# First transform of a folded FNet block: mirror sums at the norm, one pass for mirrored rows, a list by readiness, modulation by products

## The chip, the cores and the metric

The kernel runs on one core of a Trainium2 chip. The core has five engines with queues of their own: TensorE (PE, matrix products into PSUM), VectorE (DVE), ScalarE (ACT), GpSimd (POOL) and SyncE (SP, which issues most transfers). Transfers run on 16 DMA engines that all queues share. The metric is the device time in microseconds; lower is better.

## The reference

One block of a network on x (2048 rows, 512 columns), all in float32:

```python
sa, ca, ga, sb, cb, gb = (silu(c) @ w_mod).reshape(6, 512)
h = layernorm(x) * (1 + ca) + sa
a, b = h @ Wd_re.T, h @ Wd_im.T                 # 512 x 512, "hidden" transform
x = x + ga * (Ws_re @ a - Ws_im @ b)            # 2048 x 2048, "sequence" transform
h = layernorm(x) * (1 + cb) + sb
x = x + gb * ((silu(h @ w1) * (h @ w3)) @ w2)   # 1792 wide
```

The matrices Ws and Wd are those of a Fourier transform, so rows and columns have mirror images: cosines are even, sines odd. The kernel uses this (it folds rows and their mirrors together), checks on the way that the matrices given are of that kind, and has a general program behind a branch for the case that they are not.

## The kernel before, in words

The function `folded` is the main program. Tiles are taken from 50 slots of 4 KB per partition (`take`, `give`, first in, first out). Each product in full precision is three products of split operands (`PASSES`: high x high, high x low, low x high), where ScalarE rounds the high part (`copy`, L85) and VectorE makes the low part by a subtraction (`minus`, L88).

*Loads.* SyncE issues them in this order: the condition c, x rows of k = 0, the matrix of the modulation's scale (v = 1), x of k = 1, the matrix of its shift (v = 0), the four blocks of the two hidden matrices (`load_hid`, L225), x of k = 2 and 3. The rows of x are taken in eight steps k of 256: 128 rows and their 128 mirrors (`load_x`, L203 to L205; from k = 4 on the mirrors come by an indirect transfer that GpSimd issues, L168). An issue waits when eight transfers of the queue are on their way.

*Modulation.* ScalarE scales half of each matrix row by silu(c) (`copy_by`, L317), VectorE adds the other half (L292), and TensorE sums over the partitions with a column of ones (L301). This is done for four tiles, two for each of scale and shift; `mod_end` (L310) brings the sums to SBUF.

*First transform,* by k. The norm's statistics (L424, L425), root (L429), and scaling of the two tiles of rows (L444, L449); eight transposes (L464) into four PSUM banks that two k share; the modulation on the way out of PSUM (L477, L479); high and low part of the transposed rows of two k (`split_rows`). Then the hidden transform of 128 rows and of their 128 mirrors apart, in two banks (`hid_product`, L502: 24 products of 512 columns per k, three passes; `hid_odd` copies -2 times the state in between; `hid_difference`, L531: 8 products of 512 columns). Sums and differences of the two banks are taken afterwards on VectorE (`mirror_sums`, `hid_low_rows`, `hid_high_rows`), and their high and low parts are made: `us`, `ul` from the sums, `uh` from the mirrors' rows alone, of which only the high part is used. The order is written out by hand in the loop over k with the table STEPS.

*Second transform and the rest.* `seq_unit` multiplies `us`, `ul`, `uh` with the prepared blocks of the sequence matrices (L657, 32 units of 24 products). The first unit holds the last steps of the first transform (`last_rows`). Their blocks are loaded by `load_some` (L587) and prepared by `prepare_seq`. The two layers of the feed-forward part follow (L98), then the outputs' stores (L1048) and the branch to the general program.

Of the kernel before, what the change touches and what calls it, by code (L numbers as in the profile page):

```python
# [42 lines left out]
def folded(nc, pools, c, cp, wmr, wmc, x, xt, ctr, cti, wdr, wdi, w1, w3, w2, out):  # L43

# [184 lines left out]
    load_wm(1)  # L229
    load_x(1)  # L230
    load_wm(0)
# [53 lines left out]
    mod_acc = bank(6)  # L285

    def mod_scale(v):

        for h in range(2):
            w = wm[v, h]  # L290
            copy_by(w[:, 0, :], w[:, 0, :], sc[:, 2 * h : 2 * h + 1])
            nc.vector.scalar_tensor_tensor(  # L292
                w[:, 0, :], w[:, 1, :], sc[:, 2 * h + 1 : 2 * h + 2], w[:, 0, :],
                op0=OP.mult, op1=OP.add,
            )

    def mod_sum(v):

        for dt in range(ND):
            for h in range(2):  # L300
                nc.tensor.matmul(  # L301
                    mod_acc[:, v * ND + dt : v * ND + dt + 1],
                    hid_cols(wm[v, h][:, 0, :], dt),
                    onesf[:, :1],
                    start=h == 0,
                    stop=h == 1,
                )

    def mod_end(v):
        nc.vector.tensor_scalar(  # L310
            mod1[:, v, :], mod_acc[:, v * ND : (v + 1) * ND], float(v), None, op0=OP.add
        )
        for h in range(2):
            give(wm.pop((v, h)))
# [55 lines left out]
    wt, wu, wd = {}, {}, {}  # L370

    def prepare_w(dt):
# [5 lines left out]

        minus(u[:, 1, 0, :], r[:, 0, 0, :], u[:, 0, 0, :].bitcast(F32))
# [3 lines left out]
        )  # L383

# [34 lines left out]
    def norm_stats(k):  # L419
        mv = small.tile([P, 2, 2], F32, name=f"mv_{k}", tag="mv")  # L420
        rs[k] = mv, small.tile([P, 3, 2], F32, name=f"rs_{k}", tag="rs")
        for side in range(2):
            st = small.tile([P, 6], F32, name=f"st_{k}_{side}", tag="st")
            nc.vector.bn_stats(st, xz[k][:, side, :])  # L424
            nc.vector.bn_aggr(mv[:, side, :], st)  # L425
# [5 lines left out]
    def norm_scale(k):  # L431

        mv, r = rs.pop(k)
        by_scalar = (0, 1) if k in (2, 3, 4, 5) else (1,)
        nc.vector.reciprocal(r[:, 1, :], r[:, 0, :])
        first = by_scalar[0]
        nc.vector.tensor_tensor(
            out=r[:, 2, first:], in0=mv[:, first:, 0], in1=r[:, 1, first:], op=OP.mult
        )
        nc.vector.tensor_scalar(r[:, 2, first:], r[:, 2, first:], -1.0, None, op0=OP.mult)  # L440
        for side in range(2):
            a = xz[k][:, side, :]
            if side in by_scalar:
                nc.scalar.activation(  # L444
                    a, a, AF.Identity, bias=r[:, 2, side : side + 1],
                    scale=r[:, 1, side : side + 1],
                )
            else:
                nc.vector.tensor_scalar(  # L449
                    a, a, mv[:, side, 0:1], r[:, 1, side : side + 1],  # L450
                    op0=OP.subtract, op1=OP.mult,
                )


    turned = {}
    hm, hh, hl = {}, {}, {}

    def turn_rows(k):
        g, p = divmod(k, 2)
        if p == 0:  # L460
            turned[g] = [bank(dt) for dt in range(ND)]
# [1800 lines left out]
```

## Time and profile before

| | us |
|---|---|
| median of 3 runs (726.54 to 727.52) | 726.9 |
| the profiled execution | 725.83 |
| its span in the profile | 723.9 |
| first product of the second transform | 99.4 |
| second transform without a break from | 104.8 |
| TensorE busy | 695.6 |
| VectorE busy | 551.8 |
| ScalarE busy | 431.8 |

The profile takes one execution apart. "Busy" counts the time in which an engine has at least one instruction under way; products are pipelined, so that the busy time of one is longer than its distance to the next. Groups give line, engine, operation, output and inputs by their names, shape, count, then busy us and mean ns, then the idle time ahead of them with what ended it. Stretches give each engine's busy time with its instructions in brackets, TensorE's granted clock, the share of the 16 DMA engines and GB/s. The chain of waits goes back from the last instruction to what released each one; its pieces count only the time that a step adds to the chain.

### The profile page before, as it was taken

To read this page: it belongs to the slowest core of one execution; us is meant where nothing else is said; L and a number is where in the kernel's file an instruction comes from. 1 tells how busy PE (TensorE), PEld (TensorE's weight loads), DVE (VectorE), ACT (ScalarE), POOL (GpSimd) and SP (SyncE) were. 2 spreads that over 40 slices of the span, in tenths; PEclk is the share of its full clock that TensorE was granted. 3 is DMA by queue.
4 is the path that set the end of the run, shared out by engine and by line. 5 is a ranking of instruction groups with operands and counts; after the bars stand their busy time and mean duration, and the time that the engine had idled before them with its cause. 6 is when DMAs were issued, how large, how long until landed. Compare 5 with 4: busy or idle time off the path is not lost.

```text
span 723.9 us, 8651 instructions
## 1 busy us (share of the span) xinstructions
PE 695.6 (96%) x3018; PEld 562.6 (78%) x3018; DVE 551.8 (76%) x881; ACT 431.8 (60%) x684; POOL 128.2 (18%) x147
## 2 busy tenths in 40 slices
PE   7978989999999999989999999999999999999994
PEld 4666868878888888868888788777788888888784
DVE  5767788999899989758997987897666456664763
ACT  4668767535544575457566767777575655756330
POOL 2602044353343200010101001011010101101000
PEclk8889999999999999999999999999999999999998
DMA  7703059878587642162468575456944648447503
GB/s 240 225 0 117 0 173 314 313 234 317 203 294 255 237 135 70 31 115 88 74 189 163 138 166 99 104 91 144 289 87 117 146 76 185 87 90 151 141 0 121
DMA packets 37955, 108.91 MB, mean 150 GB/s; under 512 B 4880, under 2 KB 5136, under 8 KB 37904
## 3 DMA queue, kind: packets, MB, share of 16 engines
q0 software_dynamic: 12352, 43.00, 28.5%
q1 hardware_dynamic: 25552, 65.29, 27.0%
q8 instruction: 25, 0.41, 0.2%
q14 instruction: 26, 0.21, 0.1%
HBM read 76.81 MB, written 33.55 MB: 152 GB/s over the span
## 4 chain that ended last, share of the span: by engine, by line
PE 74%; DVE 11%; ACT 7%; DMA 3%; issue 2%; SPq 2%; ACTq 0%; DVEq 0%
PE bank L98 50%; PE bank L657 22%; DMA wmr<-in_wmr 1%; ACT xc L801 1%; PE bank L531 1%; DVE hl L88 1%; ACT hm L479 1%; SPq L225 1%; ACT us L85 1%; DVE xc L94 1%; PE bank L502 1%; DVE up L88 1%; DVE up L91 1%; ACT x L444 1%; ACT hf L85 1%
## 5 line engine op out<-in xcount | busy, mean ns | idle before, releaser
L98 PE MATMUL bank<-hf,w2h 128*128 128x512 f32 (+1 forms) x452 | 140.8, 391 | 0.3
L1053 POOL DMA_DIRECT2D sum<-y x48 | 41.1, 855 | 388.9 <-ACT y L317 371.8
L98 PEld LDWEIGHTS bank<-hf,w2h 128*128 128x128 f32 x452 | 84.3, 188 | 22.2 <-DVE hf L88 3.4
L98 PE MATMUL bank<-hf,w2l 128*128 128x512 f32 (+1 forms) x226 | 87.6, 388 | 0.0
L85 ACT ACTIVATE hf<-v 128x512 fp32r<-128x512 f32 x56 | 35.3, 630 | 67.7 <-DVE v L94 63.1
L317 ACT ACTIVATE y<-bank,gb 128x512 f32<-128x512 f32 x96 | 64.8, 682 | 18.1 <-PE bank L98 17.6
L91 DVE TENSOR_TENSOR v<-bank,x 128x512 f32<-128x512 f32 x36 | 24.7, 685 | 34.6 <-PE bank L98 34.6
L168 POOL DMA_INDIRECT re<-in_ctr,mirror x32 | 36.1, 1127 | 82.4 <-ACT junk L186 32.1
L657 PE MATMUL bank<-bh,us 128*128 128x512 f32 x128 | 49.9, 390 | 0.4 <-DVE xr L712 0.4
L657 PE MATMUL bank<-bh,ul 128*128 128x512 f32 x128 | 49.8, 389 | 0.0
L657 PE MATMUL bank<-l,us 128*128 128x512 f32 x128 | 49.8, 389 | 0.0
L657 PE MATMUL bank<-d,us 128*128 128x512 f32 x128 | 49.8, 389 | 0.0
L657 PE MATMUL bank<-d,uh 128*128 128x512 f32 x128 | 49.8, 389 | 0.0
L657 PE MATMUL bank<-l,uh 128*128 128x512 f32 x128 | 49.8, 389 | 0.0
L91 DVE TENSOR_TENSOR x<-bank,x 128x512 f32<-128x512 f32 x36 | 24.7, 687 | 32.4 <-PE bank L98 28.7
L98 PEld LDWEIGHTS bank<-hf,w2l 128*128 128x128 f32 x226 | 42.4, 188 | 8.3
L88 DVE TENSOR_TENSOR hf<-v,hf 128x512 fp32r<-128x512 f32 x56 | 38.4, 686 | 12.4 <-ACT hf L85 12.4
L502 PE MATMUL bank<-wu,hh 128*128 128x512 f32 x128 | 42.7, 416 | 4.9 <-ACT hh L85 3.8
L1131 ACT ACTIVATE v<-v 128x512 f32<-128x512 f32 x36 | 22.8, 632 | 38.6 <-DVE v L91 38.6
L85 ACT ACTIVATE x<-bank 128x512 f32<-128x512 f32 x72 | 41.4, 586 | 7.1 <-PE bank L98 6.5
L168 POOL DMA_INDIRECT im<-in_cti,mirror x32 | 34.4, 1076 | 35.4 <-DVE l L88 9.8
L502 PEld LDWEIGHTS bank<-wu,hh 128*128 128x128 f32 x128 | 24.8, 197 | 12.3 <-ACT hh L85 4.7
(233 smaller groups left out, 1772.0 us busy)
## 6 DMA issues: line engine op xcount, KB each, us to landing
sum<-y POOLq DMA_DIRECT2D x48, 512.0 KB, 5.4
w<-in_w SPq DMA_DIRECT2D x42, 512.0 KB, 4.7
re<-in_ctr SPq DMA_DIRECT2D x32, 256.0 KB, 4.9
im<-in_cti SPq DMA_DIRECT2D x32, 256.0 KB, 4.6
wmc<-in_wmc SPq DMA_DIRECT2D x8, 512.0 KB, 6.5
xr<-in_xt SPq DMA_DIRECT2D x8, 512.0 KB, 7.9
sum<-xr SPq DMA_DIRECT2D x8, 512.0 KB, 6.6
x<-in_x SPq DMA_DIRECT2D x12, 256.0 KB, 4.9
```

What stands on the lines that cost most here:

```text
L85: nc.scalar.activation(dst, src, AF.Copy, scale=scale)
L88: nc.vector.tensor_tensor(out=dst, in0=a, in1=b, op=OP.subtract)
L91: nc.vector.tensor_tensor(out=dst, in0=a, in1=b, op=OP.add)
L94: nc.vector.tensor_tensor(out=dst, in0=a, in1=b, op=OP.mult)
L98: nc.tensor.matmul(acc, lhs[a], rhs[b], start=first and n == 0, stop=last and n == len(PASSES) - 1, skip_group_check=more,)
L168: nc.gpsimd.indirect_dma_start(dst, None, rows, bass.IndirectOffsetOnAxis(ap=at, axis=0))
L225: nc.sync.dma_start(raw_w[dt][q * 64 : (q + 1) * 64, m, :], w[i][par::2, q])
L317: nc.scalar.activation(dst, src, AF.Identity, scale=by)
L502: nc.tensor.matmul(hb[st], lhs, wu[dt][:, b].rearrange("p a n -> p (a n)"), start=dt == 0 and n == 0, stop=dt % 2 == 1 and n == 2, skip_gr ...
L657: nc.tensor.matmul(acc[what, e], lhs, rhs, start=begin and i == 0, stop=(end or (turn and what == "x")) and i == len(terms) - 1, skip_grou ...
L1053: nc.gpsimd.dma_start(sums[t, d // 2], y, accum_op=OP.add)
L1131: behind(k != 0 or q == 0, lambda: nc.scalar.activation(v, src, AF.Silu))
```

## The change

- *Loads.* Each half block of a hidden matrix comes by one transfer of 128 partitions in place of two of 64, with the source's pattern rearranged so that the pair comes first. The shift's matrix is loaded before x of k = 1.
- *Modulation by products.* TensorE multiplies the matrix tiles as they are loaded with the columns of silu(c); ScalarE's and VectorE's scalings go, two small additions come.
- *Sums at the norm.* The sums and differences of rows and mirrors are taken right behind the modulation, in SBUF, in 512 elements each with runs of 128; the product then works on sums in the left half of a bank and differences in the right, with products of 256 columns, one bank per k, which a product with zeros clears first. The mirrors' rows are multiplied apart in one pass (three for k = 4), in two banks, with a negated copy of two blocks for the upper half.
- *The list.* Each step of the first transform is a task with what it needs, the engines that can do it, and its estimated time; `arrange` goes through them by the estimated beginning and a rank and so fixes each engine's order when the program is built. The estimated arrivals of loads are numbers in the code.
- *The branch.* The flag is read without a check of its bounds, and the skipped code is put out of the straight path.

```diff
         for m, w in enumerate((wdr, wdi)):
-            for q in range(2):
-                nc.sync.dma_start(raw_w[dt][q * 64 : (q + 1) * 64, m, :], w[i][par::2, q])
+            nc.sync.dma_start(raw_w[dt][:, m, :], w[i][par::2].rearrange("r q n -> q r n"))
...
     load_x(0)
     load_wm(1)
+    load_wm(0)
     load_x(1)
-    load_wm(0)
...
-    def mod_scale(v):
-
-        for h in range(2):
-            w = wm[v, h]
-            copy_by(w[:, 0, :], w[:, 0, :], sc[:, 2 * h : 2 * h + 1])
-            nc.vector.scalar_tensor_tensor(
-                w[:, 0, :], w[:, 1, :], sc[:, 2 * h + 1 : 2 * h + 2], w[:, 0, :],
-                op0=OP.mult, op1=OP.add,
-            )
+    def mod_sum(v, h):
 
         for dt in range(ND):
-            for h in range(2):
+            for n in range(2):
                 nc.tensor.matmul(
-                    mod_acc[:, v * ND + dt : v * ND + dt + 1],
-                    hid_cols(wm[v, h][:, 0, :], dt),
-                    onesf[:, :1],
-                    start=h == 0,
-                    stop=h == 1,
+                    mod_acc[:, 2 * v + h, dt : dt + 1],
+                    hid_cols(wm[v, h][:, n, :], dt),
+                    sc[:, 2 * h + n : 2 * h + n + 1],
+                    start=n == 0,
+                    stop=n == 1,
                 )
...
+    def mirror_sums(k, m):
+
+        if m == 0:
+            hs[k] = take(F32, "hs")
+        (minus if m else plus)(
+            sides(hs[k])[:, :, m, :], sides(hm[k])[:, :, 0, :], sides(hm[k])[:, :, 1, :]
+        )
...
+    def mirror_part(k):
+
+        h1[k] = take(F32R, "h1")
+        rows = sides(hm[k])[:, :, 1, :]
+        u = h1[k].rearrange("p a (d n) -> p a d n", d=ND)
+        copy(u[:, 0], rows)
+        if k == NK // 2:
+            minus(u[:, 1], rows, u[:, 0].bitcast(F32))
+        give(hm.pop(k))
...
+    def hid_product(k, dt):
+        if dt == 0:
+
+            hb[k] = bank(4 + k % 2)
+            nc.tensor.matmul(
+                hb[k], nought, flat(wt[0])[:, :N], start=True, stop=False, skip_group_check=True
+            )
+        for m in range(2):
+            for n, (a, b) in enumerate(PASSES):
                 nc.tensor.matmul(
-                    hb[st],
-                    lhs,
-                    wu[dt][:, b].rearrange("p a n -> p (a n)"),
...
+                    halves(hb[k])[:, m, :],
+                    sides((hh, hl)[a][k])[:, dt, m, :],
+                    wu[dt][:, b, m, :],
...
+    def hid_mirror(k, high):
+
+        h1b[k, high] = to = bank(6 + high)
+        u = h1[k].rearrange("p a (d n) -> p a d n", d=ND)
+        passes = PASSES if k == NK // 2 else PASSES[:1]
+        for dt in range(ND):
+            w = quarters(wn[dt]) if high and dt < 2 else wu[dt]
+            for n, (a, b) in enumerate(passes):
                 nc.tensor.matmul(
+                    to,
+                    u[:, a, dt, :],
+                    w[:, b].rearrange("p a n -> p (a n)"),
...
+    def arrange(hand_over=0.1, window=0.3):
+        while pending:
+            ready = []
+            for at, (rank, name, needs, fn, ways) in enumerate(pending):
+                if any(n not in ends for n in needs):
+                    continue
+                for engine, us in ways.items():
+                    begin = clear.get(engine, 0.0)
+                    for n in needs:
+                        end, by = ends[n]
+                        begin = max(begin, end if by == engine else end + hand_over)
+                    ready.append((begin, rank, us, at, engine))
+            soon = min(r[0] for r in ready) + window
+            begin, rank, us, at, engine = min(
+                (r for r in ready if r[0] <= soon), key=lambda r: (r[1], r[0] + r[2])
+            )
+            _, name, _, fn, ways = pending.pop(at)
+            ends[name] = (begin + us, engine)
+            clear[engine] = begin + us
+            fn(engine) if len(ways) > 1 else fn()
...
+    PACE = 7.5
...
+    at(13.2, "mod")
+    at(12.0, "turn0.0", "turn0.1")
+    at(13.2, "x1")
+    for dt in range(ND):
+        at(14.5 + 1.6 * dt, f"w{dt}")
+    for k in range(2, 4):
+        at(21.0 + 1.8 * (k - 2), f"x{k}")
...
+    for dt in range(ND):
+        task(f"wh{dt}", -8 + 2 * dt, [f"w{dt}"], lambda dt=dt: w_highs(dt), ACT=0.8)
+        task(f"wl{dt}", -6 + 2 * dt, [f"wh{dt}"], lambda dt=dt: w_lows(dt), DVE=0.8)
+        task(f"wd{dt}", -6 + 2 * dt, [f"wl{dt}"], lambda dt=dt: differ_w(dt), POOL=3.0)
...
+                task(
+                    f"stats{k}.{s}", r - 13 + s / 2, [f"x{k}"],
+                    lambda k=k, s=s: norm_stats(k, s), DVE=0.85,
+                )
...
+        for m in range(2):
+            task(
+                f"sum{k}.{m}", r - 8 + m, [f"mod{k}.{dt}" for dt in range(ND)],
+                lambda k=k, m=m: mirror_sums(k, m), DVE=0.61,
+            )
...
+        for n in range(2):
+            needs = [f"h1{k}", *[f"wl{dt}" for dt in range(ND)], *[f"wn{dt}" for dt in range(2)]]
...
-    with tc.If(nc.values_load(bad[0:1, 0:1], min_val=0, max_val=1) != 0):
+    flag = nc.values_load(
+        bad[0:1, 0:1],
+        min_val=0,
+        max_val=1,
+        skip_runtime_bounds_check_because="it is one less a comparison's 0 or 1",
+    )
+    with tc.If(flag != 0, preferred_fallthrough_block=False):
         general(nc, pools, *args)
```

More of the change, by code (lines that the diff above doesn't have):

```diff
@@ new lines, in folded @@
+    PACE = 7.5
+    seq_steps = []
+    keep_warm(3)
+    for side in range(2):
+        norm_stats(0, side)
+    norm_root(0)
+    norm_inverse(0)
+    for side in range(2):
+        norm_scale(0, side, "ACT" if side else "DVE")
+        turn_rows(0, side)
+    for v in (1, 0):
+        mod_sum(v, 0)
+        mod_half(v)
+        mod_sum(v, 1)
+        mod_end(v)
+    keep_warm(2)
+    give(first_tmp)
+    nc.gpsimd.memset(flat(zero), 0.0)
+    copy(nought, zero[:, 0, :P])
+    at(13.2, "mod")
@@ L1271, in folded @@
+    for dt in range(2):
+        task(f"wn{dt}", dt, [f"wl{dt}"], lambda dt=dt: w_minus(dt), ACT=1.0)
+    for n in range(6):
+        needs = [f"wd{dt}" for dt in range(ND)]
+        task(f"check{n}", 5 * PACE + n, needs, lambda n=n: check_w(n), ACT=1.0 if n < 4 else 0.4)
+    task("zz", 2 * PACE, [], clear_z, ACT=1.0)
+    for k in range(NK):
+        r = k * PACE
+        both = [f"{k}.0", f"{k}.1"]
         if k:
             for s in range(2):
-                hid_difference(2 * k - 2 + s)
```

456 lines of the change are left out of this document (236 added, 220 removed).

## The prediction

> **What bounds the kernel now.** I read the page first, then stretches of time, then the chain of waits and the timeline.
>
> ```profile
> span 723.9 us, 8651 instructions
> PE 695.6 (96%) x3018; PEld 562.6 (78%) x3018; DVE 551.8 (76%) x881; ACT 431.8 (60%) x684; POOL 128.2 (18%) x147
> ```
>
> TensorE is busy for all but 28 us. The stretches (busy us per engine, granted clock, share of the 16 DMA engines, GB/s) show where the rest lies:
>
> ```profile
> 22.50:44.00 21.50, 16.72 (x74) 12.67 (x72) 14.46 (x37) 15.63 (x28) 7.95 (x8) 0.96 0.48 150
> 44.00:52.40 8.40, 7.84 (x21) 5.89 (x22) 5.99 (x11) 3.33 (x7) 0.00 (x0) 0.59 0.00 0
> 52.40:99.40 47.00, 44.15 (x206) 35.82 (x205) 36.53 (x68) 38.41 (x63) 6.83 (x6) 1.00 0.18 58
> 104.80:160.00 55.20, 54.84 (x242) 45.04 (x241) 50.57 (x68) 34.04 (x68) 24.47 (x26) 1.00 0.86 293
> ```
>
> Up to 104.8 us, the first transform, no engine is full, and behind a stall of 3.8 us TensorE ran at a clock of 0.59:
>
> ```profile
> 44.03 0.73 PE L502 MATMUL bank<-wu,hh 128*128 128x512 f32 x2 [3.79 <-ACT hh L85]
> ```
>
> From 104.8 us on it is full, at full clock. So what the first transform gains or loses reaches the end one for one, as long as the second one's loads keep their distance to it. The chain of waits gives the seam:
>
> ```profile
> 98.93 0.60 DVE l L91
> 99.53 1.15 DVE d L91
> ...
> 102.72 2.11 PE bank L531 x8
> 104.82 21.31 PE bank L657 x94
> ```
>
> The timeline has the first L657 product at 99.38 us, and eight of them run before the 1.5 us wait and the last differences:
>
> ```profile
> 99.38 0.39 PE L657 MATMUL bank<-bh,us 128*128 128x512 f32 x1
> ```
>
> So the mark to forecast is "steady L657", now at 104.82 us.
>
> **TensorE's part.** The busy time counts overlapping products; the pitch is what costs. 94 products of 512 columns in 21.31 us are 0.227 us each. Products of 256 columns stand at the end of the program:
>
> ```profile
> 712.83 0.40 PE L98 MATMUL bank<-hf,w2h 128*128 128x256 f32 x2
> ...
> 713.06 0.28 PE L98 MATMUL bank<-hf,w2l 128*128 128x256 f32 x1
> ...
> 713.42 0.28 PE L98 MATMUL bank<-hf,w2l 128*128 128x256 f32 x1
> ```
>
> From 712.83 to 713.42 are five steps of 0.118 us, half of a long one, so halving the width is paid for in full. Before, each of the eight k has 32 long products, 7.26 us. After: 24 short ones, one that clears the bank, 8 short differences and 8 long mirrored products, 2.83 + 0.23 + 0.94 + 1.82 = 5.82 us; k = 4 has 20 long ones more, 4.5 us. Saved: 8 x 1.44 - 4.5 = 7 us, but only where TensorE is what waits are for.
>
> **VectorE's part.** These groups of the first 125 us (count, busy us, mean ns) price the new list:
>
> ```profile
> L424 DVE BATCH_NORM_STATS2 st<-x 128x6 f32<-128x512 f32 x16 | 10.8, 675 | 2.2 <-DMA x<-in_x 2.2
> ...
> L88 DVE TENSOR_TENSOR hl<-hm,hh 128x1024 fp32r<-128x1024 f32 x8 | 9.5, 1221 | 2.6 <-ACT hh L85 2.6
> ...
> L477 DVE TENSOR_SCALAR hm<-bank,mod 128x512 f32<-128x512 f32 x5 | 4.0, 805 | 0.0
> ...
> L425 DVE BATCH_NORM_AGGREGATE mv<-st 128x2 f32<-128x6 f32 x16 | 2.9, 182 | 0.6
> ...
> L88 DVE TENSOR_TENSOR l<-re 128x512 fp32r<-128x512 f32 x4 | 2.7, 684 | 0.0
> ...
> L449 DVE TENSOR_SCALAR x<-x,mv,rs 128x512 f32<-128x512 f32 x4 | 2.2, 539 | 0.0
> ```
>
> Per k: statistics 1.71, root's inverse 0.33, scaling 0.54, two modulations of half width 0.8 (an estimate, half of 805 ns), two mirror sums 1.37, the low part 1.22, and three eliminations of 512 elements 2.05: about 8.0 us, 64 us for eight, and some 10 us for the weights' low parts, the first matrix blocks and the edge. The sums read runs of 128, which no row shows; I price them as the 684 ns row and give their other bound as a rival. In the planner's own costs VectorE has 66 us of steps in 69 us, ScalarE 60: the new list is bound by VectorE. So the list, once it can run, needs some 72 us behind the modulation; what matters is when it can run.
>
> **The loads of the hidden matrices.** Before, each block comes as four transfers of 64 rows into 64 partitions. After, as two of 128 partitions, whose source is written with the pair first: two runs of 64 rows. Nothing else in the program starts its source with a dimension of two. The stretches of the start show what the laying out of a transfer does:
>
> ```profile
> 3.00:6.00 3.00, 3.00 (x4) 1.12 (x4) 1.19 (x3) 0.92 (x1) 0.05 (x1) 1.00 0.92 231
> 6.00:9.00 3.00, 2.56 (x10) 1.26 (x9) 1.50 (x6) 1.74 (x3) 0.00 (x0) 1.00 0.97 376
> 9.00:12.00 3.00, 1.65 (x13) 1.38 (x12) 2.48 (x5) 0.72 (x1) 0.00 (x0) 1.00 1.03 406
> 12.00:15.00 3.00, 2.80 (x15) 1.97 (x15) 1.50 (x6) 1.72 (x3) 0.00 (x0) 0.82 1.08 238
> 15.00:18.00 3.00, 2.62 (x13) 2.32 (x11) 2.78 (x4) 1.83 (x4) 1.79 (x2) 0.50 0.64 171
> ```
>
> At 9 to 12 us full-height loads move 406 GB/s with every DMA engine busy (25.4 GB/s each). At 12 to 15 us the half-height loads keep them as busy and move 238. So the shape, not the bytes, sets the rate. For the new shape I bound from both sides. Spread over sixteen engines, the 2.10 MB take 5.2 us at 406 GB/s. Dealt out by the leading dimension, only two engines work: 50.8 GB/s, 41.3 us. I take two, since the half-height row already shows rate lost to a narrow shape and a count of two cannot be dealt further if dealing goes by the outermost dimension; this is the weakest step, and its chance below says so.
>
> The Trainium skill, "DMA: Bandwidth & Descriptors", section "Why a DMA increments its semaphore by 16 and not by 1", says that the engines of a copy are the largest number up to 16 that divides the slowest dimension of both sides, and its rules for kernel authors say that an outermost dimension below 16 confines the copy to that many. By it these loads run on two engines and the sum stands; without it sixteen engines give the first rival. No run here shows it yet.
>
> **The sum.** Ahead of the eight loads lie 3.15 MB (x of k = 0 and 1, 1.05, and the modulation's matrices, 2.10). By the rows above 3 x (231 + 376 + 406) us GB/s = 3.04 MB are moved by 12 us, so the matrices start at 12 us and the fourth block is in at 12.0 + 41.3 = 53.3 us. The list gives every engine a fixed order. ScalarE's stands at the highs of block 3 and VectorE's at its lows; behind them wait the norm roots of k = 2, the modulation of k = 1 and all mirrored products, which need every block. The two x loads after them stand behind them in the same queue. Only 11 to 12 us of VectorE's list are listed ahead of that point; behind it are 13 sums (8.9), 12 statistics (10.3), 7 low parts (8.5), 22 eliminations (15.1), 11 modulations (4.4), scalings and inverses (5.2), the matrix steps (6.5) and the weights' and the edge's (3.6): 62.5 us. The last 1.3 us lie behind the last product. So the last product ends at 53.3 + 62.5 - 1.3 = 114.5, taken as 115 us. Eight long products (1.8 us) cover the last eliminations and eight short differences (1.0 us) follow, no wait between: steady at 118 us, 13.2 later than 104.82; with a slow clock behind a wait of that length, as at 44 us, I take 14.
>
> The modulation loses four scalings on each of ScalarE and VectorE:
>
> ```profile
> L301 PE MATMUL bank<-tmp,wmr 128*128 128x1 f32 x32 | 5.9, 307 | 1.7 <-DVE wmr L292 1.7
> ...
> L292 DVE SCALAR_TENSOR_TENSOR wmr<-wmr,sc 128x512 f32<-128x512 f32 x4 | 3.0, 751 | 2.8 <-ACT wmr L317 2.8
> ...
> L317 ACT ACTIVATE wmr<-wmr,sc 128x512 f32<-128x512 f32 x4 | 2.9, 718 | 0.8 <-DMA wmr<-in_wmr 0.8
> ...
> L310 DVE TENSOR_SCALAR mod<-bank 128x4 f32<-128x4 f32 x2 | 0.2, 156 | 0.6 <-PE bank L301 0.6
> ```
>
> Its 32 products stay, with the condition's columns as the moving side; two small additions come. With its matrices in at 12 us, half of the products (3 us) put its end near 15 us, where the timeline now has 20.2:
>
> ```profile
> 19.96 0.23 DVE L310 TENSOR_SCALAR mod<-bank 128x4 f32<-128x4 f32 x2 [0.58 <-PE bank L301]
> ```
>
> The wait for the hidden matrices swallows these 5 us (in the first rival they count). SyncE issues eight transfers fewer, and the modulation's second matrix passes x of k = 1: hidden likewise.
>
> The branch at the end: nothing works behind 717.9 us, but the run lasts to 723.9.
>
> ```profile
> 717.90:723.90 6.00, 0.00 (x0) 0.00 (x0) 0.00 (x0) 0.00 (x0) 0.00 (x0) 0.50 0.02 7
> ```
>
> Putting the skipped code out of line may save between nothing and a part of these 6 us, and could cost as much as a fetch now hidden; I take -1, bounds -3 and +1.
>
> The profiled execution took 725.83 us, 1.93 more than its span; 725.83 + 14 - 1 = 738.8. The runs' median is 1.1 above that execution: 740 us. Its own range: VectorE's steps overlap (the chain above has 0.60 and 1.15 us where the groups have 684 and 1217 ns), which can take 6; an engine at 376/16 = 23.5 GB/s, as at 6 to 9 us, adds 3; waits between engines add 0 to 5: 734 to 748. An engine at the 14.9 GB/s of the half-height row would make it 70 us instead of 41; I leave that out, because there sixteen engines share 64 partitions.
>
> **Rivals.**
>
> *Sixteen engines (not slower).* Place: the eight matrix loads. Price: 5 us instead of 41. The blocks are in by 12.0 + 5.2 = 17 us, the modulation ends near 15 us, and VectorE's 74 us of list with some 4 % of waits end the first transform at 87 us, steady at 90: 15 less than now, 710.5 by the same sum, 711 to 712 on the runs' scale, 705 to 717. For it: every transfer shown used all sixteen. Against: none shown has this shape. Point from which it decides: with -1 for the branch, equal time needs the fourth block at 53.3 - 13 = 40 us, 28 us for 2.10 MB, 75 GB/s, three engines' worth. Four engines make the kernel faster.
>
> *Sixteen engines, but the list is longer than its prices (the change saves little of what its counts say).* If the sums over runs of 128 cost twice 684 ns (16 x 0.68 = 11 us on the bound engine), or each of some 40 hand-overs a quarter of a microsecond more, the first rival gives back 10 to 11 us: 722, range 717 to 729. For it: steps that follow one another on two engines leave VectorE only 36.53 of 47.0 us busy now. Against: the list has other work at hand in nearly every wait.
>
> **How the numbers follow.** Two engines 0.58, sixteen with the list as priced 0.30, sixteen with a longer list 0.12. Faster by over 0.2 % (1.5 us, about what a measurement of this kernel can tell): 0.30 and 0.07 of the last; within 0.2 %: 0.02; slower: 0.58 and 0.03. Cases of both signs hold the chance, so the range is wide: 708 to 748 takes nine tenths of the first case, most of the second and all of the third, 0.85 in all; the likeliest's own is 734 to 748.
>
> **What would show it.** The hidden-matrix loads in the list of issues: 10 us and more to landing and rising, DMA share near an eighth at some 50 GB/s from 13 to 50 us, and ScalarE idle for the matrices; against that, landings of 3 to 5 us and a share near 1. Then the first L657 product: 115 us, or 87. L502 with half-width products at 0.118 us pitch shows TensorE's part. Whatever the case, after steady L657 the stretches must be full as now; if they are not, the second transform's loads came late and the argument of one for one is wrong. The prediction fails if the landings are short.

## The result, and the profile after

The changed kernel takes 748.3 us (median of 4 runs, 747.29 to 749.39), the kernel before, on the same chip, 726.7 us: ratio 1.0297, 95% interval 1.0278 to 1.0316. The forecast was 740.0 us, its range 708 to 748. So the side and the mechanism were the forecast ones, and the time was 8.3 us over the forecast, just outside the range. One run of the last kernel below (the other order with the old branch) took 982.35 us at a granted clock of 0.65; it is left out of that kernel's figures.

The profiled execution took 749.39 us. The first two lines of its page, the span and the busy time of each engine:

```profile
span 747.5 us, 8859 instructions
...
PE 700.2 (94%) x3140; PEld 572.2 (77%) x3140; DVE 548.8 (73%) x873; ACT 426.4 (57%) x694; POOL 127.6 (17%) x147
```

TensorE's busy time hardly differs from before (695.6), and what it is not busy grew from 28 to 47 us. The stretches (length, busy us of PE, PEld, DVE, ACT, POOL, granted clock, share of the DMA engines, GB/s) say where:

```profile
12.00:15.00 3.00, 3.00 (x15) 3.00 (x15) 0.00 (x0) 0.00 (x0) 0.00 (x0) 0.50 0.18 70
15.00:30.00 15.00, 13.51 (x46) 10.30 (x46) 6.39 (x15) 4.05 (x7) 3.49 (x4) 0.50 0.14 51
30.00:40.00 10.00, 2.31 (x7) 1.42 (x6) 0.68 (x2) 1.35 (x3) 2.35 (x3) 0.50 0.13 50
...
55.85:123.30 67.45, 61.17 (x375) 53.43 (x376) 59.35 (x112) 54.91 (x106) 13.99 (x13) 0.95 0.21 69
126.30:300.00 173.70, 173.70 (x765) 143.35 (x765) 156.82 (x219) 92.47 (x180) 59.96 (x58) 1.00 0.74 252
```

From 15 to 40 us the core's loads run at 50 GB/s with an eighth of its DMA engines. Of TensorE's 13.51 us up to 30 us over half are the modulation's one-column products, at a clock of 0.50; from 30 to 40 us no compute engine has much to do. Then, from the landing of the fourth block, comes a dense stretch of 67 us, and from 126.3 us TensorE is full, as it was from 104.8 us before. The chain of waits shows the same seam:

```profile
29.89 5.09 SPq L226
35.03 20.82 DMA w<-in_wdi
...
58.21 1.01 DVE hm L478 x2
...
123.48 1.84 PE bank L714 x8
125.32 0.95 PE bank L541 x8
126.27 1.84 PE bank L714 x8
```

SyncE gets rid of one load of 256 KB in 5.09 us, 51 GB/s. The last one lands at 55.85 us. The steady second transform (L714 here, L657 before) begins at 126.27 instead of 104.82 us: 21.45 us later. From there to the last VectorE instruction it is 611.3 us (737.56 - 126.27) against 610.0 us (714.84 - 104.82), and behind that instruction 9.5 against 8.6 us. 21.45 + 1.3 + 0.9 is the whole growth of the span, 23.6 us. The 1.3 us lie inside what this part differs by between the kernels below, where it takes 609.6 to 613.5 us.

### The profile page after: what moved, and what is told of

The parts are those of the page before. It is cut to its first block, busy times and chain, and to the rows that moved or that the text cites. A ratio compares the mean times of both kernels' runs of the same rounds, so it can differ in the third digit from the quotient of the medians.

```text
span 747.5 us, 8859 instructions
## 1 busy us (share of the span) xinstructions
PE 700.2 (94%) x3140; PEld 572.2 (77%) x3140; DVE 548.8 (73%) x873; ACT 426.4 (57%) x694; POOL 127.6 (17%) x147
## 4 chain that ended last, share of the span: by engine, by line
PE 70%; DVE 7%; issue 6%; ACT 6%; SPq 4%; DMA 4%; POOL 0%; POOLq 0%; ACTq 0%; DVEq 0%
PE bank L100 45%; PE bank L714 24%; SPq L226 4%; DMA w<-in_wdi 3%; DMA sum<-y 1%; DVE hm L478 1%; DVE hl L90 1%; ACT xc L858 1%; ACT y L308 1%; ACT hm L476 1%; DVE hs L93 1%; DVE st L424 0%; PE bank L560 0%; POOL sum L1110 0%; DVE ul L90 0%
## 5 line engine op out<-in xcount | busy, mean ns | idle before, releaser
L87 ACT ACTIVATE hf<-v 128x512 fp32r<-128x512 f32 x56 | 35.3, 630 | 67.1 <-DVE v L96 62.5
L714 PE MATMUL bank<-d,us 128*128 128x512 f32 x128 | 49.9, 390 | 0.0
L714 PE MATMUL bank<-bh,us 128*128 128x512 f32 x128 | 49.9, 390 | 0.0
L714 PE MATMUL bank<-bh,ul 128*128 128x512 f32 x128 | 49.8, 389 | 0.0
L714 PE MATMUL bank<-l,us 128*128 128x512 f32 x128 | 49.8, 389 | 0.0
L714 PE MATMUL bank<-d,uh 128*128 128x512 f32 x128 | 49.8, 389 | 0.0
L714 PE MATMUL bank<-l,uh 128*128 128x512 f32 x128 | 49.8, 389 | 0.0
L524 PE MATMUL bank<-wu,hh 128*128 128x256 f32 x128 | 27.1, 306 | 13.7 <-ACT ho L87 10.4
L524 PEld LDWEIGHTS bank<-wu,hh 128*128 128x128 f32 x128 | 22.4, 204 | 17.8 <-ACT ho L87 11.8
```

What stands on the lines that cost most here:

```text
L87: nc.scalar.activation(dst, src, AF.Copy, scale=scale)
L524: nc.tensor.matmul(halves(hb[k])[:, m, :], sides((hh, hl)[a][k])[:, dt, m, :], wu[dt][:, b, m, :], start=False, stop=dt % 2 == 1 and n == ...
L714: nc.tensor.matmul(acc[what, e], lhs, rhs, start=begin and i == 0, stop=(end or (turn and what == "x")) and i == len(terms) - 1, skip_grou ...
```

## The experiments

They were taken on one core in four launches, on four chips, each beside the kernel before; so kernels of different launches are compared by their ratios to it. Line numbers shift by a few between kernels: L714, L720 and L657 are the same products of the second transform.

**1. The loads: how many engines, and what that costs.** Four kernels. The first loads as before the change:

```diff
-            nc.sync.dma_start(raw_w[dt][:, m, :], w[i][par::2].rearrange("r q n -> q r n"))
+            for q in range(2):
+                nc.sync.dma_start(raw_w[dt][q * 64 : (q + 1) * 64, m, :], w[i][par::2, q])
```

> The kernel after, with each hidden-matrix block loaded as before in four transfers of 64 rows into 64 partitions; all else as after. Two-engine theory (the loads alone cost the time): at the 238 GB/s of the half-height row the 2.10 MB take 8.8 us and the fourth block is in near 21 us. The list then starts behind the modulation (23.4 us) instead of at 55.9 us. If it takes 61.5 us as predicted, the second transform is steady near 90 us and the time is 712 us; if it takes the 67.6 us that the kernel after showed, and the part listed ahead is no longer hidden, steady at 97 to 103 us, 720 to 726 us. List theory (the list itself is what costs, the loads were hidden): above 740 us.

The second lays the same numbers out in DRAM so that a block's rows follow one another:

```diff
-            nc.sync.dma_start(raw_w[dt][:, m, :], w[i][par::2].rearrange("r q n -> q r n"))
+            nc.sync.dma_start(raw_w[dt][:, m, :], w[i, par])
...
+        w = np.asarray(w).reshape(D, ND // 2, 2, P // 2, 2)
+        return w.transpose(1, 4, 2, 3, 0).reshape(ND // 2, 2, P, D)
```

> The kernel after, with the hidden matrices laid out in DRAM so that the 128 rows of a block follow one another with no pair in front; each block is two full-height transfers, as after. Two-engine theory: leading dimension 128, sixteen engines, some 400 GB/s, 2.10 MB in 5.2 us, fourth block in near 18 us; the end is then set by the modulation and the list, so no more than 3 us faster than with half-height loads: 710 to 724 us. If it is the size of a transfer, or the merging of four into two, and not the pair in front that confines the loads, they stay near 50 GB/s and the time near 748 us.

The third lays them out so that the source starts with four instead of two:

```diff
+            nc.sync.dma_start(raw_w[dt][:, m, :], w[i, par].rearrange("j g n -> g j n"))
...
+        w = w.transpose(1, 4, 2, 3, 0).reshape(ND // 2, 2, 4, 32, D)
+        return w.transpose(0, 1, 3, 2, 4)
```

> The kernel after, with the hidden matrices laid out in DRAM so that each load's source starts with a dimension of four (4 runs of 32 rows) instead of two. Dealing by the leading dimension: four engines, about 101 GB/s, 2.10 MB in 20.6 us, fourth block in near 33 us, 23 us earlier than in the kernel after. The prediction's break-even point (fourth block at 40 us, three engines' worth) then says faster than before, about 720 us; with the 70.4 us that the kernel after took from the fourth block to steady, it says steady at 103 us, 726 us, the same as before. If the rate goes by the narrowness of the runs (32 rows instead of 64) and not by the number in front, the loads are as slow as in the kernel after or slower: 748 us or more. If a small leading dimension is no limit: as with the rows one after another.

The fourth is the kernel before with the merged load alone:

```diff
-            for q in range(2):
-                nc.sync.dma_start(raw_w[dt][q * 64 : (q + 1) * 64, m, :], w[i][par::2, q])
+            nc.sync.dma_start(raw_w[dt][:, m, :], w[i][par::2].rearrange("r q n -> q r n"))
```

> The kernel before, with only the hidden-matrix loads merged as in the change (source with the pair in front, two transfers a block). Two-engine theory: the fourth block comes near 54 us instead of 25.5 us, and the first transform's second half products wait for it; 3.8 us of that lie in the stall at 44 us anyway, so 24 to 29 us are lost: 750 to 757 us, more than the whole change loses, because the rest of the change saves some. If the loads are not the cause: 727 us.

Measured: half-height loads 724.9 us (ratio 0.9981, 0.9968 to 0.9995), rows one after another 724.3 (0.9968, 0.9955 to 0.9981), a leading four 729.3 (1.0048, 1.0033 to 1.0063), the merged load alone 754.5 (1.0388, 1.0369 to 1.0408). The stretches behind 12 us, first of the rows one after another, then of the leading four:

```profile
12.00:18.00 6.00, 5.49 (x26) 5.36 (x25) 0.33 (x2) 0.00 (x0) 4.22 (x6) 0.50 1.05 390
```

```profile
18.00:22.00 4.00, 3.75 (x19) 3.66 (x18) 0.16 (x1) 0.00 (x0) 2.32 (x3) 0.50 0.26 101
```

A leading two gives a share of 0.13 and 50 GB/s, a leading four 0.26 and 101, a leading 128 all sixteen engines and 390. That is 24 to 25 GB/s an engine each time, and the number of engines is the number in front, up to sixteen. The transfers of all three have the same 256 KB, and the shorter runs (32 rows instead of 64) came with the higher rate, so neither the size nor the length of a run explains it. This is the rule of the Trainium skill, "DMA: Bandwidth & Descriptors", section "Why a DMA increments its semaphore by 16 and not by 1", which the forecast weighed; the traces agree. The number of engines is not all: the half-height loads, whose outermost dimension is 64, keep every engine busy and yet move only 245 GB/s.

```profile
12.00:15.00 3.00, 2.82 (x14) 2.73 (x13) 0.15 (x1) 0.00 (x0) 0.06 (x1) 0.50 1.07 245
```

The merged load alone loses 28 us, more than the whole change. The chain with the leading four gives the price of a late block:

```profile
19.68 16.44 DMA w<-in_wfi
...
106.54 174.32 PE bank L714 x768
```

The last load lands at 36.1 us and the second transform is steady at 106.5, 70.4 us later. With the leading two it is 126.27 - 55.85 = 70.4 us as well. So in this range a microsecond of load is a microsecond of time. By an estimate from these figures the break-even point lies at a fourth block near 32 us (104.8 - 70.4, less the 2.2 us by which the rest of the program grew), not at the 40 us of the forecast, and four engines make the kernel slower, not faster.

Both kernels with sixteen engines are a little faster than before, but some 13 us slower than the first rival's 711 to 712 us. The rest of the runs look for these 13 us, and for the 6 us that the list behind the late blocks took too long.

**2. The modulation.** In the timeline with the rows one after another, the one-column products and the last VectorE step of the modulation:

```profile
9.69 2.36 PE L292 MATMUL bank<-sc,wmr 128*128 128x1 f32 x16
...
19.96 3.57 PE L292 MATMUL bank<-sc,wmr 128*128 128x1 f32 x16 [0.26 <-DVE mod L302]
...
23.57 0.16 DVE L93 TENSOR_TENSOR mod<-bank,mod 128x4 f32<-128x4 f32 x1 [3.66 <-PE bank L292]
```

There are 64 of them, not 32: leaving out the scalings leaves two unscaled halves to multiply. They end at 23.6 us, later than before the change (20.2). Three kernels on the basis of the row loads: the old modulation (scaled halves, 32 products),

```diff
-    for v in (1, 0):
-        mod_sum(v, 0)
-        mod_half(v)
-        mod_sum(v, 1)
-        mod_end(v)
+    for v in (1, 0):
+        mod_scale(v)
+        mod_sum(v)
+    for v in (1, 0):
+        mod_end(v)
```

> The kernel after with the hidden matrices laid out row after row, and the modulation as before: the matrices scaled on ScalarE and VectorE, then 32 products of one column instead of 64. Theory that the modulation is the second loss: with row loads alone it ends at 23.6 us, because 64 products of one column run at a clock of 0.50 and are handed over four times; with half the products it ends near 17 to 19 us and the whole list moves up by 5 to 6 us: 718 to 720 us, against 724.3 with row loads alone. Theory that the list's own waits and TensorE's slow clock set the end: no change, 724 us.

all four parts summed up on ScalarE and VectorE first, 8 products (with five instead of two products of 512 columns around them, whose results nobody reads),

```diff
+        copy_by(a, a, sc[:, 0:1])
+        for n in range(1, ND):
+            nc.vector.scalar_tensor_tensor(
+                a, wm[v, n // 2][:, n % 2, :], sc[:, n : n + 1], a, op0=OP.mult, op1=OP.add
+            )
```

> As the kernel with the modulation as before, but all four parts of each matrix are added up on ScalarE and VectorE first (one scaling and three steps of 0.75 us for each of the two), and only 8 products of one column are left; products of 512 columns between them keep TensorE's clock up. Theory that the modulation sets the start of the list: it ends near 16 us, 7.5 us earlier than with row loads alone: 716 to 718 us. Theory that it does not: 724 us.

and the modulation as in the change, but the planner told of its true end:

```diff
-    at(13.2, "mod")
+    at(23.6, "mod")
...
+    clear["PE"] = 23.6
```

> The kernel after with the hidden matrices laid out row after row, and the planner told that the modulation ends at 23.6 us and that TensorE is busy until then, instead of 13.2 us; nothing else. VectorE, idle from 9 to 23.6 us in row loads alone, then has the statistics and the matrices' low parts listed ahead of the modulation: up to 8 us of its 68 us list move into the idle time: 717 to 720 us if VectorE's list sets the end; 724 us if the modulation's products set it in another way (TensorE's or ScalarE's list).

Measured: old modulation 721.5 us (0.9925, 0.9908 to 0.9943), summed-up 719.2 (0.9902, 0.9885 to 0.9920), later plan 724.7 (0.9976, 0.9961 to 0.9992). Where the modulation ends in the first two:

```profile
17.16 0.23 DVE L311 TENSOR_SCALAR mod<-bank 128x4 f32<-128x4 f32 x2 [4.28 <-PE bank L302]
```

```profile
14.94 0.23 DVE L309 TENSOR_SCALAR mod<-bank 128x4 f32<-128x4 f32 x2 [1.19 <-PE bank L298]
```

It ends 6.3 and 8.6 us earlier than with the 64 products, and the kernels gain some 3 and 5 us by it. So modulation by products is a loss once the loads are quick; in the changed kernel the late blocks hide it. The later plan was an edit that could not do what was expected: the modulation's own four additions stand in VectorE's queue ahead of everything the planner lists, and VectorE still waited 14.7 us for them. It says nothing on the theories.

**3. What sets the length of the list.** The forecast had VectorE's work set it. Three kernels on the basis of the summed-up modulation: two take work off one engine each, the third changes the list. Less work on VectorE:

```diff
-        nc.vector.bn_stats(st, xz[k][:, side, :])
+        nc.vector.bn_stats(st, xz[k][:, side, :64])
```

> The kernel with summed-up modulation matrices, whose norm statistics read only the first 64 of 512 columns of each row (the statistics of the other 448 columns are left out): 14 VectorE instructions of 0.68 us behind the modulation shrink to some 0.15 us, 7.4 us less on VectorE, nothing else changed. VectorE theory (its list sets the end of the first transform, as the prediction had it): 719.2 - 7 = 712 us. Waits theory (the chain of hand-overs between engines sets it, VectorE's 7.8 us of idle time only move): 716 to 719 us.

Less work on TensorE:

```diff
-            for n, (a, b) in enumerate(PASSES):
+            for n, (a, b) in enumerate(TWO):
...
+    TWO = [p for p in PASSES if p != (0, 1)]
```

> The kernel with summed-up modulation matrices, with two instead of three short products for each part of the first transform (the product with the low part of the matrix is left out): 64 of 192 products of 256 columns at 0.118 us, 7.6 us less on TensorE, in the first transform alone. If TensorE is not what waits are for there, as the prediction had it: 717 to 719 us. If it is: 712 us.

The same steps in another order (six of some 30 edits of this kind; the ranks come from a lay-out with the durations of the traces). With other durations the planner also chooses the engine anew where a step can run on two:

```diff
-    def arrange(hand_over=0.1, window=0.3):
+    def arrange(hand_over=0.35, window=0.3):
...
-    at(13.2, "mod")
+    at(15.2, "mod")
...
-                    f"stats{k}.{s}", r - 13 + s / 2, [f"x{k}"],
+                    f"stats{k}.{s}", r - 17.7 + s / 2, [f"x{k}"],
...
-                lambda e, k=k, dt=dt: modulate_rows(k, dt, e), ACT=0.36, DVE=0.36,
+                lambda e, k=k, dt=dt: modulate_rows(k, dt, e), ACT=0.5, DVE=0.5,
...
-            task(f"hh{k}", r - 6.5, sums_done, lambda k=k: sum_highs(k), ACT=0.97)
+            task(f"hh{k}", r - 8.43, sums_done, lambda k=k: sum_highs(k), ACT=0.97)
...
-        task(f"ul{k}", r + 6, [f"us{k}"], lambda k=k: low_columns(k, 1), DVE=0.61)
+        task(f"ul{k}", r + 1.99, [f"us{k}"], lambda k=k: low_columns(k, 1), DVE=0.61)
```

> The kernel with summed-up modulation matrices, the same steps with the same operations, but listed by other ranks and by the durations and arrival times that the traces show (modulation at half width 0.5 us, a hand-over of 0.35 us, matrices from 13.7 us). Laid out with the measured durations this order ends the first transform 7 us earlier. Waits theory (8 us of VectorE's time behind the loads were waits which the listed order made): 712 to 715 us. If the waits come from the machine and not from the order: 719 us.

Measured: short statistics 718.7 us (0.9882, 0.9863 to 0.9901), two passes 719.2 (0.9896, 0.9875 to 0.9918), other order 712.9 (0.9805, 0.9789 to 0.9821). The same stretch of each, in the order: summed-up basis, short statistics, two passes, other order.

```profile
15.20:92.70 77.50, 67.94 (x401) 57.55 (x400) 69.73 (x131) 61.03 (x119) 21.14 (x20) 0.93 0.28 92
```

```profile
15.20:92.70 77.50, 68.02 (x404) 58.12 (x404) 63.95 (x133) 60.73 (x120) 20.94 (x21) 0.94 0.30 94
```

```profile
15.20:92.70 77.50, 60.55 (x332) 50.66 (x332) 69.12 (x131) 60.19 (x118) 20.03 (x19) 0.91 0.26 90
```

```profile
15.20:85.00 69.80, 61.55 (x396) 55.88 (x395) 66.94 (x127) 59.02 (x118) 18.79 (x18) 0.93 0.29 95
```

VectorE has 5.8 us less to do in the second row, TensorE 7.4 us less in the third, and the end does not move (steady at 95.2 and 96.0 us, 95.6 in the basis). Neither engine's work alone sets it. In the fourth row VectorE is busy 96% of the time instead of 90%, and the steady point is 88.5 us, 7 us earlier. The stretch is 7.7 us shorter: 4.9 us less in which VectorE waits (2.9 instead of 7.8) and 2.8 us less of its work. That work is less in part because ScalarE took over seven of its modulations, while VectorE got three more scalings. The modulations on VectorE in the basis and in the other order:

```profile
L484 DVE TENSOR_SCALAR hm<-bank,mod 128x256 f32<-128x256 f32 x15 | 7.5, 537 | 2.6 <-ACT hm L482 2.2
```

```profile
L484 DVE TENSOR_SCALAR hm<-bank,mod 128x256 f32<-128x256 f32 x8 | 4.0, 538 | 0.4 <-ACT hm L482 0.2
```

Since 5.8 us less work on VectorE gained nothing under the old order, it is the list, the order together with the choice of engines, that was worth the 7 us; the two were not tried apart. With the early loads the waits theory holds, and the forecast's premise falls. No run takes work off ScalarE alone.

Does the same hold in the changed kernel, whose blocks come late? The next one leaves its loads and modulation alone and tells the planner the true times:

```diff
-    at(13.2, "mod")
+    at(23.4, "mod")
...
-        at(14.5 + 1.6 * dt, f"w{dt}")
+        at((22.6, 33.4, 43.9, 55.9)[dt], f"w{dt}")
...
-        at(21.0 + 1.8 * (k - 2), f"x{k}")
+        at(51.0 + 5 * (k - 2), f"x{k}")
```

> The kernel after, loads on two engines left as they are, but the planner told when things really come (modulation 23.4 us, matrix blocks 22.6, 33.4, 43.9 and 55.9 us, instead of 13.2 and 14.5 to 19.3 us) and the longer durations that the trace shows. A lay-out of the kernel after with measured durations gives its measured end (differences end at 126.3 us); the same lay-out of the new order ends at 112 to 114 us. Order theory (behind the late loads 13 us are lost because the fixed order is made for early ones): 735 us. Theory that VectorE's work behind the fourth block sets the end whatever the order: 748 us.

Measured 747.6 us (1.0288, 1.0270 to 1.0307): no gain that shows. The new order made a wait of its own, as VectorE's row, SyncE's issues and a piece of the chain show:

```profile
60.78 0.69 DVE L424 BATCH_NORM_STATS2 st<-x 128x6 f32<-128x512 f32 x1 [14.98 <-DMA x<-in_x]
```

```profile
38.76 7.91 SPq L205 DMA_DIRECT2D x<-in_x  x1
46.72 0.69 SPq L207 DMA_DIRECT2D x<-in_x  x1
47.45 1.11 SPq L205 DMA_DIRECT2D x<-in_x  x1
48.60 0.81 SPq L207 DMA_DIRECT2D x<-in_x  x1
49.46 8.59 SPq L205 DMA_DIRECT2D x<-in_x  x4
```

```profile
49.46 11.30 DMA x<-in_x
```

VectorE waits 15 us for a transfer issued at 49.46 us. It is the fifth of the x loads behind the matrices, after two each for k = 2 and 3, so it brings rows of k = 4. The plan had listed their statistics ahead of those of k = 2: it lets the rows from k = 4 on come 6 us behind GpSimd's issue and knows nothing of SyncE's queue. The rows of k = 2, which I had put at 51 us, landed at 58.1 and 58.8 us by the trace's records of landings. Behind the wait this order has 55.5 us of VectorE's work and 5.8 us of its waits left:

```profile
60.78:122.08 61.30, 54.57 (x351) 49.59 (x351) 55.54 (x108) 47.58 (x96) 6.58 (x6) 0.91 0.16 52
```

So the two engines hold up more than the matrices, and this run does not decide between the theories: whether another order would shorten the list behind late blocks stays open. How the time would go with early rows and late matrices was not tried.

**4. The branch at the end.** The edit alone in the kernel before (first diff), and the old branch in three kernels of the change (second diff):

```diff
-    with tc.If(nc.values_load(bad[0:1, 0:1], min_val=0, max_val=1) != 0):
+    flag = nc.values_load(
+        bad[0:1, 0:1],
+        min_val=0,
+        max_val=1,
+        skip_runtime_bounds_check_because="it is one less a comparison's 0 or 1",
+    )
+    with tc.If(flag != 0, preferred_fallthrough_block=False):
```

> The kernel before, with only the edit of the branch at the end (the skipped code out of line, no bounds check of the flag). The prediction's step: 1 us less, bounds -3 and +1. The theory from the kernel after, whose stretch behind the last VectorE instruction grew from 8.6 to 9.5 us: 0.9 us more. If it is nothing: 726 us as before.

```diff
-    with tc.If(flag != 0, preferred_fallthrough_block=False):
+    with tc.If(nc.values_load(bad[0:1, 0:1], min_val=0, max_val=1) != 0):
```

> The kernel with summed-up modulation matrices, with the branch at the end as before the change. Prediction's step (1 us saved by the edit; the edit alone in the kernel before measured 0.7 us saved): 720 us, 0.7 to 1 us slower than with the edit. If the longer stretch behind the last VectorE instruction in all kernels with the change (9.4 to 10.1 us against 8.6 us) comes from the edit in this larger program: 718.3 us.

> The kernel after with the branch at the end as before. If the edit saves what it saved alone in the kernel before (0.7 us; the prediction had 1 us): 749 us. If it costs in the longer program, as the stretch behind the last VectorE instruction says (9.5 us with the edit, 7.7 us with the old branch in the kernel with summed-up matrices): 746.5 to 747.5 us.

> The kernel in the other order (summed-up matrices, rows one after another) with the branch at the end as before. If the edit costs 1 to 2 us in the longer program: 711 to 712 us against 712.9 us with the edit. If the edit saves 0.7 us: 713.6 us.

Measured: the edit alone 725.7 us (0.9991, 0.9982 to 0.9999). The old branch: in the summed-up kernel 718.5 (0.9882, 0.9860 to 0.9903; with the edit 0.9902), in the changed kernel 748.0 (1.0297, 1.0279 to 1.0314; with the edit the same ratio), in the other order 709.1 (0.9767, 0.9752 to 0.9783; with the edit 0.9805, 0.9789 to 0.9821). The last VectorE instruction of the changed kernel with the edit (span 747.5 us) and with the old branch (span 746.4 us):

```profile
737.56 0.48 DVE L1101 SCALAR_TENSOR_TENSOR xr<-bank,gb,xr 128x256 f32<-128x256 f32 x1 [0.63 <-PE bank L100]
```

```profile
738.40 0.48 DVE L1101 SCALAR_TENSOR_TENSOR xr<-bank,gb,xr 128x256 f32<-128x256 f32 x1 [0.63 <-PE bank L100]
```

The same of the other order with the edit (span 711.8 us) and with the old branch (span 707.2 us):

```profile
702.01 0.48 DVE L1107 SCALAR_TENSOR_TENSOR xr<-bank,gb,xr 128x256 f32<-128x256 f32 x1 [0.63 <-PE bank L100]
```

```profile
699.54 0.48 DVE L1107 SCALAR_TENSOR_TENSOR xr<-bank,gb,xr 128x256 f32<-128x256 f32 x1 [0.63 <-PE bank L100]
```

The stretch behind that instruction is 7.5 and 7.2 us with the old branch, against 9.5 and 9.3 us with the edit (737.56 + 0.48 to 747.5; 702.01 + 0.48 to 711.8). So it is in all the changed programs: 9.3 to 10.1 us with the edit, 7.2 to 7.7 us with the old branch. In the kernel before it is 8.1 us with the edit and 8.6 us without, but 7.8 us in the one with the merged load alone, which has the old branch too; so by the stretch the edit is not told from nothing there. The timed runs have it 0.7 us faster, at the edge of their interval, so that its sign is another there is not shown. The edit costs some 2 us of the stretch in the changed programs, but only in the other order do the timed runs show a loss, of about 2.8 us. In that profiled pair the spans differ by 4.6 us, of which 2.1 lie in the stretch; the rest lies ahead of it, where the two programs are the same. What makes the stretch longer was not found.

The other order with the old branch is the fastest kernel of the study: 709.1 us, 17 us faster than before.

## Why the prediction was wrong, step by step

The mechanism was right. Two DMA engines carry the matrix loads, they delay the first transform, the list behind them is fixed, and the delay reaches the end one for one. What failed were the sizes of four terms. On the scale of the profiled executions the forecast was 738.8 us and the result 749.39: 10.6 us, of which 7.45 lie ahead of the steady point (21.45 instead of 14), 1.9 in the branch's stretch and 1.3 in between. The 7.45 are 2.5 for the fourth block and 6.4 for the list behind it, less 1.5 us that the forecast had to spare between the last product and the steady point (4.3 against 2.8, its rounding and its slow clock).

*The fourth block at 53.3 us.* It came at 55.85. The rate of 50.8 GB/s nearly held: by the trace's records the first six loads of 256 KB landed 5.2 us apart, 50 GB/s. The last two, with x loads issued behind them from 38.7 us on, took 6 us each, which is 1.5 of the 2.5 us; the rest is the slightly lower rate and a start 0.6 us later. Why the last two were slower was not found.

*The list behind it, 62.5 us of VectorE's work less 1.3.* This step failed, and it is the largest term: the last product came 67.6 us behind the fourth block (123.48 - 55.85) instead of 61.2. The work was priced well in sum: VectorE is busy for 59.35 us of that stretch. The groups of the stretch in the changed kernel:

```profile
L424 DVE BATCH_NORM_STATS2 st<-x 128x6 f32<-128x512 f32 x12 | 8.2, 680 | 0.0
L478 DVE TENSOR_SCALAR hm<-bank,mod 128x256 f32<-128x256 f32 x13 | 6.5, 536 | 12.4 <-ACT hm L476 11.6 <-issue 0.4
L93 DVE TENSOR_TENSOR hs<-hm 128x512 f32<-128x512 f32 x7 | 4.8, 692 | 1.8 <-ACT hm L476 1.6
...
L90 DVE TENSOR_TENSOR hs<-hm 128x512 f32<-128x512 f32 x7 | 4.8, 682 | 0.0
```

The sums over runs of 128 cost the 684 ns that they were priced at, so the second rival's first reason is out. The half-width modulation costs 0.54 us and not 0.40, and there are 13 and not 11 of them: 6.5 us instead of 4.4, which other steps made up for. What was missing is 8.1 us in which VectorE waits (67.45 - 59.35): 2.4 us until ScalarE has done what stands ahead of its modulation (to 58.21 us), and 5.7 us in many small waits later. I had taken the sum of the bound engine's work for the length of the list, with 0 to 5 us of waits only in the range. The runs put something else in its place: with early loads less work on VectorE or on TensorE does not move the end, and another list does. For late blocks the trace shows the waits, but what would remove them stays open. The forecast saw that the rows of k = 2 stand behind the matrices and gave them no time of their own; in the changed kernel's own order that cost nothing (no wait ahead of L424 in the groups above).

*The branch, -1.* In the changed program the stretch at the end grew by 0.9 us, inside the bounds of -3 to +1. The timed runs of the changed kernel with and without the edit do not tell it from nothing.

*The modulation's end near 15 us and its 32 products.* 64 products, ended at 23.4 us. The count was misread: with the condition on the moving side, each of the two unscaled halves needs its own product. The late blocks hid it, as the forecast said, and so it cost nothing in the changed kernel.

Right was the pitch of the short products, here 0.12 us each (three starts, of an x2, an x1 and the next x2)

```profile
64.95 0.40 PE L524 MATMUL bank<-wu,hh 128*128 128x256 f32 x2
65.19 0.28 PE L524 MATMUL bank<-wu,hl 128*128 128x256 f32 x1
65.31 0.40 PE L524 MATMUL bank<-wu,hh 128*128 128x256 f32 x2
```

Right were also the two steps from the last product to the steady point (eight long products from 123.48 us, eight short differences from 125.32 to 126.27 us), and the full stretches behind it.

*The first rival* (sixteen engines, 711 to 712 us) was tried for itself and gave 724.3. Its miss is the modulation (23.6 us instead of 15), 2.8 us more list than the 75 us that it gave between modulation and steady (101.37 - 23.6 = 77.8), and about 2 us at the end. A steady point near the rival's 90 us (88.5) appeared only after both the modulation and the list had been changed. *The second rival's* 722 us is near by luck: of its two reasons the dear sums are excluded, the list came out only 2.8 us longer than the first rival had it, and the largest part of the first rival's miss, the modulation's 8.6 us, is in neither reason.

## What to carry to other kernels

When transfers are merged, read the outermost dimension of the new source and destination: an eight-fold gap in rate hangs on it, and a host layout with the rows first gives the merge without the loss. The busy sum of the fullest engine is a lower bound for a stage of dependent steps, not its length; here another order and choice of engines was worth 7 of 77 us with the same steps. An order drawn up for arrivals that don't come true can be redrawn from the trace, but with every transfer and its queue in it: the one redrawn here for the late blocks left SyncE's queue out and gained nothing. Removing an operation can double another: count the products that are left, not those that were there.

## What the runs showed of the hardware

One-column products ran at half clock here after some 2 us, although TensorE was busy 3.57 of 3.70 us. With the row loads, sixteen took 2.36 us at first (9.69 us) and 3.57 us later, 0.22 us each. The granted clock by stretch:

```profile
9.60:10.60 1.00, 1.00 (x12) 1.00 (x10) 0.00 (x0) 0.00 (x0) 0.00 (x0) 1.00 1.01 406
10.60:11.60 1.00, 1.00 (x8) 1.00 (x8) 0.00 (x0) 0.00 (x0) 0.00 (x0) 0.70 1.02 393
...
12.30:16.00 3.70, 3.57 (x16) 3.49 (x16) 0.09 (x1) 0.00 (x0) 2.31 (x4) 0.50 1.05 391
```

Some of VectorE's additions were slower while GpSimd computed. In the kernel with the old modulation, the second row runs beside GpSimd's three additions (the first row); a like one of VectorE, with GpSimd idle, takes 0.69 us (the third).

```profile
18.78 3.00 POOL L400 TENSOR_TENSOR wd<-w 128x256 fp32r<-128x256 f32 x3
...
19.98 1.21 DVE L90 TENSOR_TENSOR hs<-hm 128x512 f32<-128x512 f32 x1
...
29.59 0.69 DVE L93 TENSOR_TENSOR hs<-hm 128x512 f32<-128x512 f32 x1
```

The two mirror sums beside GpSimd's work took 0.95 and 1.21 us, the other fourteen 0.68 to 0.69. That GpSimd is the cause was not tried by itself.

And a queue's full-width transfers behind two-engine ones are late with them. In the changed kernel the first x load of k = 2, issued at 38.68 us behind the eight matrix loads, has sixteen marks of landing in the trace: fourteen came at 48.2 to 48.6 us, the last two at 56.3 and 56.5 us, just behind the last matrix (55.85 us).
